# The last 64 rows of d in two weight gradients: half-array pairs in w2's gradient, and the same form at the beginning of w1's

## The chip, the cores and the metric

The kernel runs on one core of a Trainium2 chip. The metric is the device time of one execution in microseconds (us). Three runs of the kernel before took 354.17, 354.51 and 356.31 us; the median is 354.51. The engines are named as in the profile: PE (TensorE, matmuls), PEld (its weight loads), DVE (VectorE), ACT (ScalarE), POOL (GpSimd) and SP (SyncE, which issues most loads).

## The reference

One layer with two branches, forward and backward. The first branch is a layer norm, a real two-dimensional FFT over 2048 x 448, a product with complex weights and the inverse FFT; the second is a layer norm and an MLP over the 2048 tokens.

```python
def _B_ref(x, w1, b1, w2, b2):                      # x: 1 x 2048 x 448
    h = _layernorm(x, axis=-1)
    u = jnp.einsum("bsd,sf->bdf", h, w1) + b1       # f: 1792
    u = _gelu(u)
    y = jnp.einsum("bdf,fs->bds", u, w2) + b2
    return y.transpose(0, 2, 1)

h = x + irfft2(rfft2(_layernorm(x)) * (w_r + 1j * w_i))
h2 = h + _B_ref(_layernorm(h), w1, b1, w2, b2)
_out, _vjp = jax.vjp(f, A_x, A_w_r, A_w_i, B_w1, B_b1, B_w2, B_b2)
```

The kernel returns `h2` and the seven gradients for a given `grad_out`. Two of them matter here, both sums over the 448 values of d: w2's gradient (out_6, 1792 x 2048), the product of gelu(u) and `grad_out`, and w1's gradient (out_4, 2048 x 1792), the product of the normed h and the gradient of u.

## The kernel before

The program is not written in the order in which it runs. Each step is recorded as an operation with the buffers that it reads and writes, the engines that can take it and planned durations; `Plan.order` (from line 266) then lays all operations out by priority, and what each engine gets is a fixed list. Buffers come from rings. The ring "ps" stands for the eight PSUM banks, and `caps` (line 448) limits how many banks each kind of user holds: "mm" 4, "sp" (all transforms) 5, "mw" 8. `_room` (line 211) answers when a further bank of a kind is free. PE's lists keep operations of one "mode" together, since the plan counts 0.095 us for a change between the whole array and halves of it.

The order of the work, roughly: from 0 to 75 us of the span the forward FFT, with products for the gradient of gelu as filler (kind "mg"); to 175 us the two MLP products (kind "mp"); to 219 us the product of w1 with the gradient of u (kind "mm", 16 row tiles), each row followed by the layer norm's backward step `norm_back` on DVE and ACT (lines 1181 to 1207); from 219 to 306 us the backward FFT (`fft_rows`, `fft_cols`, `ifft_cols`, `ifft_rows`, kind "sp"), with w2's gradient as filler; and from 298 us w1's gradient.

Both gradients sum over d = 448, that is three full tiles of 128 rows and 64 rows over. The operands are turned by DMA so that d lies on the partitions: `g_t` and `goT` for w2's gradient, `hlnT` and `du_t` for w1's. Each has four planes of 128 rows; the fourth is loaded from columns 320 to 447, so that its upper half (partitions 64 to 127) holds the last 64 rows of d.

- w2's gradient (lines 1276 to 1285): 14 row tiles of 128, each of four banks of 512 columns. A bank takes four matmuls on the whole array. So that the fourth counts 64 rows alone, POOL zeroes the lower half of `g_t`'s fourth plane (line 1249). ACT moves the banks out.
- w1's gradient (lines 1308 to 1336): 16 row tiles of 128, each of four banks of 448 columns, kind "mw". A bank takes three matmuls on the whole array (`whole`); the last 64 rows run on half of the array (`tails`): a DMA copies the upper half of the fourth plane to the lower half (lines 1250 to 1251), and of two banks one takes its 64 rows from the lower, one from the upper half of the partitions, so that two matmuls run side by side. Even row tiles go whole, whole, tails, odd ones tails, whole, whole, so that the tails of two neighbours meet.

`norm_back` keeps its three small columns (the accumulated sum and two factors) in one tile, "nm". `Norm.moments` (line 705) works in the tile "mv_h", into which the operation before it accumulates.

Of the kernel before, what the change touches and what calls it, by code (L numbers as in the profile page):

```python
# [18 lines left out]
P = 128  # L19
# [118 lines left out]
class Plan:  # L138
# [71 lines left out]
    def _room(self, b, nth):  # L210

        spec = self.rings[b.ring]
        if spec.get("fifo") and spec["next"] + nth != b.seq:
            return None
        ends = sorted(s for s in spec["slots"] if s is not None)
        if len(ends) <= nth:
            return None
        best = ends[nth]
        cap = spec.get("caps", {}).get(b.kind)
        if cap is not None:  # L220
            live = sorted(float("inf") if x.left else x.end for x in spec["live"].get(b.kind, []))
            if len(live) >= cap:
                t = live[len(live) - cap]
                if t == float("inf"):
                    return None
                best = max(best, t)
        return best
# [170 lines left out]
def evict(n):  # L398
    return on_act(n) + on_dve(n)
# [8 lines left out]
def kernel(  # L408
# [39 lines left out]
    ring("ps", 8, ps, fifo=False, caps={"mm": 4, "mg": 2, "sp": 5, "mw": 8, "mp": 6})  # L448
# [24 lines left out]
    ncol = [0]  # L473

# [104 lines left out]
    def turn(j, w2n):  # L579
        for a in range(0, NT, 8):  # L580
            pt = bank("sp", [P, 8, P], BF16)

            def go(e, on, a=a, pt=pt):
                for t in range(8):
                    e.transpose(pt[:, t], w2n[:, (a + t) * P:(a + t + 1) * P], ident[:])

            pl.op(mm(*[128] * 8), go, r=[w2n, ident], w=[pt])
            copy(on_act(1024) + [("DVE", 1.13, 1.21)], lambda a=a: w2T[j][:, a:a + 8, :], lambda pt=pt: pt[:], [pt], [(w2T[j], a)])
# [76 lines left out]
    class Norm:  # L665
# [9 lines left out]
        def stats(self, h):  # L675
            bs = col(6, f"bs_{self.nm}")
            if h % self.by == 0:
                self.mv = col(3 * self.by, f"mv_{self.nm}")
            mv, i, n = self.mv, h % self.by, self.by
            pl.op(on_dve(448, 1.0e-3, 0.07), lambda e, on: e.bn_stats(out=bs[:], in_=self.src[:, h, :]),  # L680
                  r=[(self.src, h)], w=[bs])
            pl.op(small(), lambda e, on: e.bn_aggr(out=mv[:, 2 * i:2 * i + 2], in_=bs[:]), r=[bs], w=[(mv, i)])
            if i == n - 1:
                self.close(h, mv, self.scale)
# [20 lines left out]
        def moments(self, h):  # L705

            mv, i = self.mv, h % self.by
            pl.op(small(), lambda e, on: e.tensor_scalar(
                out=mv[:, 2 * i:2 * i + 1], in0=mv[:, 2 * i:2 * i + 1], scalar1=1.0 / D, scalar2=None, op0=ALU.mult),
                r=[(mv, (i, 0))], w=[(mv, (i, 0))])  # L710
            sq = k1([P, D], "sq")
            pl.op([("ACT", 0.66, 0.8)], lambda e, on: e.activation(
                out=sq[:], in_=self.src[:, h, :], func=ACT.Square, scale=-1.0, bias=mv[:, 2 * i:2 * i + 1],
                accum_out=mv[:, 2 * i + 1:2 * i + 2]), r=[(self.src, h), (mv, (i, 0))], w=[sq, (mv, (i, 1))])
            if i == self.by - 1:
                self.close(h, mv, self.scale / D)
# [37 lines left out]
    def fft_rows(src, zt, g, on_pe):  # L754
# [25 lines left out]
        for i, h in enumerate(hs):  # L780
            pz = bank("sp", [P, 4, 32, 4])
            if on_pe:
                calls = [(512, lambda pz=pz, n=n: pz[0:n], lambda h=h, k=k: src[:, h, parts[k]], signs[k], k == 0, k == 3)
                         for k, n in enumerate((113, 112, 112, 113))]
                matmuls(pz, calls, [(src, h), (src, (h, 1)), kf])
            else:
                matmuls(pz, [(128, lambda c=c, pz=pz: pz[0:DC, c], lambda c=c, i=i: w[:, i, c, :], lambda: kf[:, 0, :],
                              True, True) for c in range(4)], [w, (kf, 0)])
            copy(evict(512), lambda h=h: zt[:, :, :, 4 * h:4 * h + 4], lambda pz=pz: pz[0:DC], [pz], [(zt, h)])
# [3 lines left out]
    def fft_cols(zt, dtab, dst):  # L793
# [4 lines left out]
        def step1(j):  # L798
            pr = bank("sp", [P, 4, DC])
# [20 lines left out]
        def step2(j):  # L820
            px = bank("sp", [P, 2, DF])
# [60 lines left out]
    def ifft_cols(ys, ab):  # L882

        for a in (7, 6, 5, 4, 3, 2, 1, 8):
            two = (a, 16 - a) if a < 8 else (8, 0)
            pa, pb = (bank("sp", [P, 2, 2, 2, 64]) for _ in range(2))
# [42 lines left out]
    def ifft_rows(ab, itab, h):  # L929
        pq = bank("sp", [P, 2, 2, DC])  # L930
# [14 lines left out]
        py = bank("sp", [P, D])  # L945
# [58 lines left out]
    for h in range(NT):  # L1004
        with grouped():
            py = ifft_rows(ab, di0, h)
            if h % nh.by == 0:
                nh.mv = col(3 * nh.by, "mv_h")
            mv, i = nh.mv, h % nh.by
            pl.op([("DVE", 0.54, 0.68)], lambda e, on, py=py, h=h, mv=mv, i=i: e.tensor_tensor_reduce(  # L1010
                out=hn[:, h, :], in0=py[:], in1=hn[:, h, :], scale=1.0, scalar=0.0, op0=ALU.add, op1=ALU.add,
                accum_out=mv[:, 2 * i:2 * i + 1]), r=[py, (hn, h)], w=[(hn, h), (mv, (i, 0))])
            nh.moments(h)
# [167 lines left out]
    def norm_back(pb, xhat, xkey, h, nm, base, out, okey):  # L1181


        nms = col(3, "nm")
# [3 lines left out]
            op1=ALU.add, accum_out=nms[:, 0:1]), r=[pb, xkey, nm.rneg], w=[junk, (nms, 0)])  # L1188
        v = pl.buf("f2", [P, D], "v", F32)
        if nm.raw:  # L1190
            by = 1
            pl.op([("DVE", 0.075, 0.17)], lambda e, on: e.tensor_scalar(  # L1192
                out=nms[:, 1:3], in0=nm.rn[:, h, :], scalar1=nms[:, 0:1], scalar2=None, op0=ALU.mult),
                r=[(nms, 0), (nm.rn, (h, 0)), (nm.rn, (h, 1))], w=[(nms, 1), (nms, 2)])
        else:
            by = 0
            pl.op([("DVE", 0.131, 0.213)], lambda e, on: e.tensor_scalar(
                out=nms[:, 2:3], in0=pb[:, D:D + 1], scalar1=nm.rn[:, h, 0:1], scalar2=-1.0 / D, op0=ALU.mult,
                op1=ALU.mult), r=[pb, (nm.rn, (h, 0))], w=[(nms, 2)])
        pl.op([("ACT", 0.53, 0.64)], lambda e, on: e.activation(  # L1200
            out=v[:], in_=pb[:, 0:D], func=ACT.Identity, scale=nm.rn[:, h, 0:1], bias=nms[:, 2:3]),
            r=[pb, (nms, 2), (nm.rn, (h, 0))], w=[v])
        pl.op([("DVE", 0.595, 0.68)], lambda e, on: e.scalar_tensor_tensor(  # L1203
            out=junk[:], in0=xhat(), scalar=nms[:, by:by + 1], in1=v[:], op0=ALU.mult, op1=ALU.add),
            r=[xkey, (nms, by), v, junk], w=[junk])
# [6 lines left out]
    def ld_t4(t, src, r):  # L1212
        n = t.shape[2]
        ld_parts(t, [0], lambda b: b[:, 0:3, :], lambda: src()[:, 0:384], P * 3 * n * 2, True, r)
        ld_parts(t, [1], lambda b: b[:, 3, :], lambda: src()[:, 320:448], P * n * 2, True, r)

# [4 lines left out]
    ld_t4(goT, lambda: grad_out[0], [])  # L1221
# [27 lines left out]
    pl.op([("POOL", 0.6, 0.7)], lambda e, on: e.memset(g_t[0:64, 3, :], 0.0), w=[(g_t, 1)])  # L1249
    for t in (hlnT, du_t):  # L1250
        st(lambda t=t: t[0:64, 3, :], lambda t=t: t[64:128, 3, :], 64 * t.shape[2] * 4, [(t, 1)], [(t, 2), (t, 1)])

# [22 lines left out]

    for j in range(NFB):
        s6 = pl.buf("w4", [P, S], "s6")
        with grouped():
            for n in range(4):
                pw = product("mm", 512, [(lambda c=c, j=j: g_t[:, c, j * P:(j + 1) * P],  # L1280
                                          lambda c=c, n=n: goT[:, c, 512 * n:512 * n + 512],
                                          [(g_t, c // 3), (goT, c // 3)]) for c in range(4)], [P, 512], hold=s6)
                copy(on_act(512), lambda s6=s6, n=n: s6[:, 512 * n:512 * n + 512], lambda pw=pw: pw[:], [pw], [(s6, n)])
                pl.ops[-1].level = 300.0
# [23 lines left out]
    last = None  # L1308
    for h in range(NT):
        s4 = pl.buf("w4", [P, F], "s4")  # L1310
        bs = [bank("mw", [P, 448]) for _ in range(4)]

        def call(n, rows_, c, start, stop, h=h, bs=bs):
            return (448, lambda: bs[n][:], lambda: hlnT[rows_, c, h * P:(h + 1) * P],
                    lambda: du_t[rows_, c, 448 * n:448 * n + 448], start, stop)

        def whole(h=h, bs=bs, s4=s4):
            return [matmuls(bs[n:n + 2], [call(m, slice(0, P), c, c == 0 and h % 2 == 0,
                                               c == 2 and h % 2 == 1) for m in (n, n + 1) for c in range(3)],
                            [(hlnT, 0), (du_t, 0), (s4, ("held", 0))]) for n in (0, 2)]  # L1320

        def tails(h=h, bs=bs, s4=s4):
            return [matmuls(bs, [call(n + i, (LO, UP)[i], 3, h % 2 == 1, h % 2 == 0) for n in (0, 2) for i in range(2)],
                            [(t, k) for t in (hlnT, du_t) for k in (1, 2)] + [(s4, ("held", 0))], mm(448, 448), "rows")]

        with grouped():
            for o in tails() + whole() if h % 2 else whole() + tails():
                if last is not None:
                    o.soft.add(last.idx)
                last = o  # L1330
            for n in range(4):
                copy(evict(448), lambda s4=s4, n=n: s4[:, 448 * n:448 * n + 448], lambda bs=bs, n=n: bs[n][:], [bs[n]],
                     [(s4, n)])
                pl.ops[-1].level = 300.0
# [52 lines left out]
```

## Time and profile before

| | |
|---|---|
| runs | 354.17, 354.51, 356.31 us, median 354.51 |
| the profiled execution | 354.65 us, span 352.9 us |
| mean granted clock of PE | 0.99 |
| PE waits, by releaser | DMA of w2n 8.7 us (once, at the start), ACT v 4.0 (twice), DVE rneg_x 1.1, and seven under 0.8 |
| evictions of w2's gradient | 56 on ACT, 588 ns each |
| evictions of w1's gradient | 38 on ACT, 538 ns; 26 on DVE, 624 ns |
| `norm_back`'s v on ACT | 725 ns, 16 in the MLP's part |
| zeroing of g_t's half plane on POOL | 1585 ns, once |
| copies of a half plane on POOL's queue | hlnT issued at 252.8 us, landed after 3.7; du_t at 273.0, after 3.5 |

How to read it: the profile is of one execution, made by the hardware profiler, and times are counted from the span's start. A group's line gives what it writes and reads, its shape and count, then its busy time, the mean length of one and the idle time of the engine before it with what ended that. Matmuls overlap in the array: one that lasts 353 ns from start to end can start 190 ns after the one before, so PE's work is read from starts and not from lengths. The chain of waits that ended last is short here: PE with w1's gradient from 306.75 us for 37.83 us, then the last evictions and stores.

### The profile page before, as it was taken

To read this page: it belongs to the slowest core of one execution; us is meant where nothing else is said; L and a number is where in the kernel's file an instruction comes from. 1 tells how busy PE (TensorE), PEld (TensorE's weight loads), DVE (VectorE), ACT (ScalarE), POOL (GpSimd) and SP (SyncE) were. 2 spreads that over 40 slices of the span, in tenths; PEclk is the share of its full clock that TensorE was granted. 3 is DMA by queue.
4 is the path that set the end of the run, shared out by engine and by line. 5 is a ranking of instruction groups with operands and counts; after the bars stand their busy time and mean duration, and the time that the engine had idled before them with its cause. 6 is when DMAs were issued, how large, how long until landed. Compare 5 with 4: busy or idle time off the path is not lost. (4 is left out here: it accounts for less than half of the span.)

```text
span 352.9 us, 6853 instructions
## 1 busy us (share of the span) xinstructions
PE 331.7 (94%) x2507; PEld 180.6 (51%) x2507; DVE 270.4 (77%) x755; ACT 196.8 (56%) x419; POOL 71.7 (20%) x124
## 2 busy tenths in 40 slices
PE   0979999999999999999999999599999999999994
PEld 0546555666655555555555555255555655444441
DVE  5798999886579994422277776859998999997652
ACT  2797833575588776306012222588777887655332
POOL 0000000074701101123220100001111233276522
PEclk9999999999999999999999999699999999999999
DMA  7999799999999999999999999299521555377654
GB/s 239 386 236 210 161 185 298 221 204 294 312 310 316 302 233 306 196 337 261 170 253 241 203 255 248 61 267 236 168 104 81 197 204 201 145 248 246 238 196 156
DMA packets 134685, 80.49 MB, mean 228 GB/s; under 512 B 94268, under 2 KB 127164, under 8 KB 134524
## 3 DMA queue, kind: packets, MB, share of 16 engines
q1 hardware_dynamic: 127148, 52.71, 66.8%
q0 software_dynamic: 7504, 27.35, 22.1%
q8 instruction: 19, 0.31, 0.4%
q14 instruction: 14, 0.11, 0.1%
HBM read 30.98 MB, written 27.08 MB: 165 GB/s over the span
## 5 line engine op out<-in xcount | busy, mean ns | idle before, releaser
L518 PE MATMUL ps_mm<-goT,g_t 128*128 128x512 bf16 x224 | 56.8, 391 | 4.0 <-ACT v L1200 4.0
L518 PE MATMUL ps_mg<-go_n,w2T 128*128 128x448 bf16 x224 | 49.4, 355 | 1.6 <-DMA go_n<-in_grad_out_dram 0.7
L518 PE MATMUL ps_mw<-du_t,hlnT 128*128 128x448 bf16 (+1 forms) x256 | 45.3, 353 | 0.6 <-ACT v L1200 0.5
L518 PE MATMUL ps_mm<-du,w1T 128*128 128x449 bf16 x224 | 43.3, 353 | 0.0
L518 PE MATMUL ps_mp<-hln,w1c 128*128 128x448 bf16 x224 | 42.9, 352 | 0.0
L518 PE MATMUL ps_mp<-gT,w2c 128*128 128x448 bf16 x224 | 42.7, 352 | 0.0
L1200 ACT ACTIVATE v<-ps_mm,nm,rn_h 128x448 f32<-128x448 f32 x16 | 11.6, 725 | 48.7 <-DVE nm L1186 46.7
L508 ACT CAST s<-ps_mm 128x512 bf16<-128x512 f32 x56 | 32.7, 588 | 10.5 <-PE ps_mm L518 10.3
L500 POOL DMA_DIRECT2D out_dram<-s x31 | 16.9, 546 | 91.3 <-ACT s L508 69.1
L518 PEld LDWEIGHTS <-g_t 128*128 128x128 bf16 x224 | 20.3, 100 | 25.3 <-issue 7.4
L518 PEld LDWEIGHTS <-hlnT 128*128 128x128 bf16 (+1 forms) x256 | 20.6, 97 | 24.1 <-issue 6.9
L518 PEld LDWEIGHTS <-w1T 128*128 128x128 bf16 x224 | 21.8, 97 | 21.1
L518 PEld LDWEIGHTS <-w2c 128*128 128x128 bf16 x224 | 21.9, 98 | 20.5
L518 PEld LDWEIGHTS <-w1c 128*128 128x128 bf16 x224 | 21.9, 98 | 20.3
L508 ACT CAST s<-ps_mw 128x448 bf16<-128x448 f32 x38 | 18.6, 538 | 22.9 <-PE ps_mw L518 19.3
L518 PEld LDWEIGHTS <-w2T 128*128 128x128 bf16 x224 | 19.5, 97 | 17.5 <-issue 1.6
L510 DVE CAST s<-ps_mw 128x448 bf16<-128x448 f32 x26 | 15.9, 624 | 10.2 <-PE ps_mw L518 8.3
L1168 DVE SCALAR_TENSOR_TENSOR h<-ps_mp,b2c,hr 128x448 bf16<-128x448 f32 x16 | 9.8, 677 | 16.8 <-PE ps_mp L518 16.8
L816 DVE TENSOR_TENSOR gg<-ps_sp,gb 128x226 bf16<-128x226 f32 x60 | 19.9, 411 | 2.5 <-ACT gb L508 2.5
L1203 DVE SCALAR_TENSOR_TENSOR junk<-hln,nm,v 128x448 bf16<-128x448 bf16 x16 | 10.9, 684 | 11.8 <-ACT v L1200 11.8
L1081 DVE SCALAR_TENSOR_TENSOR ge<-ge 128x448 bf16<-128x448 bf16 x14 | 8.7, 620 | 13.4 <-ACT ge L1079 13.4
L500 POOL DMA_DIRECT2D hn_d<-x x4 | 2.5, 614 | 75.5 <-DVE rn_h L695 71.3
(129 smaller groups left out, 584.1 us busy)
## 6 DMA issues: line engine op xcount, KB each, us to landing
w2c<-in_B_w_dram SPq DMA_DIRECT2D x8, 896.0 KB, 10.6
out_dram<-s POOLq DMA_DIRECT2D x14, 512.0 KB, 3.2
out_dram<-s POOLq DMA_DIRECT2D x15, 448.0 KB, 2.8
w1c<-in_B_w_dram SPq DMA_DIRECT2D x6, 1024.0 KB, 9.3
x<-in_A_x_dram SPq DMA_DIRECT2D x4, 448.0 KB, 7.0
go_n<-in_grad_out_dram SPq DMA_DIRECT2D x2, 896.0 KB, 10.8
hn_d<-x POOLq DMA_DIRECT2D x4, 448.0 KB, 5.8
hln_d<-hln POOLq DMA_DIRECT2D x4, 448.0 KB, 7.4
```

The costliest lines, as they stand in the source:

```text
L500: e.dma_start(out=out() if callable(out) else out, in_=in_())
L508: e.copy(out=out(), in_=in_())
L510: e.tensor_copy(out=out(), in_=in_())
L518: e.matmul(out(), lhsT=lhsT(), rhs=rhs(), start=start, stop=stop)
L816: pl.op(on_dve(226), lambda e, on, s_=s_, op=op: e.tensor_tensor(out=g_[:, s_, :].rearrange("p (k t) -> p t k", t=2), in0=pr[:, 0:2, :], i ...
L1081: gop(stt, [q_, uf], [zz], lambda e, g: e.scalar_tensor_tensor(out=g(zz), in0=g(q_), scalar=6.0 * GELU_C, in1=g(uf), op0=ALU.add, op1=ALU. ...
L1168: pl.op([("DVE", 0.595, 0.68)], lambda e, on, t=t, p2=p2, h2=h2: e.scalar_tensor_tensor(out=h2[:], in0=p2[:, 0:D], scalar=b2c[:, t:t + 1], ...
L1200: pl.op([("ACT", 0.53, 0.64)], lambda e, on: e.activation(out=v[:], in_=pb[:, 0:D], func=ACT.Identity, scale=nm.rn[:, h, 0:1], bias=nms[:, ...
L1203: pl.op([("DVE", 0.595, 0.68)], lambda e, on: e.scalar_tensor_tensor(out=junk[:], in0=xhat(), scalar=nms[:, by:by + 1], in1=v[:], op0=ALU. ...
```

## The change

The core of the diff; the same kind of edit repeated is left out:

```diff
-            if len(live) >= cap:
-                t = live[len(live) - cap]
+            if len(live) + nth >= cap:
+                t = live[len(live) + nth - cap]
...
-    ring("ps", 8, ps, fifo=False, caps={"mm": 4, "mg": 2, "sp": 5, "mw": 8, "mp": 6})
+    ring("ps", 8, ps, fifo=False, caps={"mm": 4, "mg": 2, "sp": 5, "sb": 4, "mw": 8, "mp": 6})
...
-        def moments(self, h):
+        def moments(self, h, sm):
+            if h % self.by == 0:
+                self.mv = col(3 * self.by, f"mv_{self.nm}", bufs=2)
...
-        nms = col(3, "nm")
+        nm2 = col(1, "nm2", bufs=3)
+        ab = col(2, "nm1", bufs=3)
...
-    def ld_t4(t, src, r):
+    def ld_t4(t, src, r, cuts=1):
         n = t.shape[2]
-        ld_parts(t, [0], lambda b: b[:, 0:3, :], lambda: src()[:, 0:384], P * 3 * n * 2, True, r)
         ld_parts(t, [1], lambda b: b[:, 3, :], lambda: src()[:, 320:448], P * n * 2, True, r)
+        for k in range(cuts):
+            at = slice(k * n // cuts, (k + 1) * n // cuts)
+            ld_parts(t, [(0, i) for i in range(4 * k // cuts, 4 * (k + 1) // cuts)], lambda b, at=at: b[:, 0:3, at],
+                     lambda at=at: src()[at, 0:384], P * 3 * n * 2 // cuts, True, r)
+        st(lambda: t[0:64, 3, :], lambda: t[64:128, 3, :], 64 * n * 4, [(t, 1)], [(t, 2), (t, 1)])
...
-    ld_t4(goT, lambda: grad_out[0], [])
+    ld_t4(goT, lambda: grad_out[0], [], 2)
...
-    pl.op([("POOL", 0.6, 0.7)], lambda e, on: e.memset(g_t[0:64, 3, :], 0.0), w=[(g_t, 1)])
-    for t in (hlnT, du_t):
-        st(lambda t=t: t[0:64, 3, :], lambda t=t: t[64:128, 3, :], 64 * t.shape[2] * 4, [(t, 1)], [(t, 2), (t, 1)])
+    sp[0] = "sb"
...
+    behind, EARLY = [], 6
+    def outer(kind, a_t, b_t, j, width, dst, turn, evict_):
+        bs = [bank(kind, [P, width]) for _ in range(4)]
+        held = [(dst, ("held", 0))]
+        begins = (lambda n: n < 2) if turn is None else (lambda n: turn == 0)
+        def call(n, rows_, c, start, stop):
+            return (width, lambda: bs[n][:], lambda: a_t[rows_, c, j * P:(j + 1) * P],
+                    lambda: b_t[rows_, c, width * n:width * n + width], start, stop)
...
+        def tails():
+            return matmuls(bs, [call(n + i, (LO, UP)[i], 3, not begins(n), begins(n)) for n in (0, 2) for i in range(2)],
+                           [(t, k) for t in (a_t, b_t) for k in (1, 2)] + held, mm(width, width), "rows")
+        with grouped():
+            if turn is None:
+                os = [whole(0), whole(1), tails(), whole(2), whole(3)]
+            elif turn == 0:
+                os = [whole(0, 1), whole(2, 3), tails()]
+            else:
+                os = [tails(), whole(0, 1), whole(2, 3)]
+            for o in os:
+                if behind:
+                    o.soft.add(behind[-1].idx)
+                behind.append(o)
...
-            for n in range(4):
-                pw = product("mm", 512, [(lambda c=c, j=j: g_t[:, c, j * P:(j + 1) * P],
-                                          lambda c=c, n=n: goT[:, c, 512 * n:512 * n + 512],
-                                          [(g_t, c // 3), (goT, c // 3)]) for c in range(4)], [P, 512], hold=s6)
+        outer("mm", g_t, goT, j, 512, s6, None, on_act(512))
...
+        outer(*(("mm",) if h < EARLY else ("mw",)), hlnT, du_t, h, 448, s4, None if h < EARLY else h % 2, evict(448))
```

What it does, part by part:

- Both gradients are made by one function, `outer`. In w2's gradient the last 64 rows of d now run as two half-array pairs per row tile: bank 0 whole, bank 1 whole, the tails of all four banks, bank 2 whole, bank 3 whole. `g_t` and `goT` get the copy of the half plane that `hlnT` and `du_t` had; the zeroing of `g_t` goes.
- The first six row tiles of w1's gradient take the same form and the bank kind "mm"; the other ten keep "mw" and the alternation. All row tiles of both gradients stand in one sequence (`behind`).
- The backward transforms have a bank kind of their own, "sb", with four banks instead of five. `_room` counts the banks that the same operation has already asked for.
- `ld_t4` loads the fourth plane first, and `goT`'s first three planes in two pieces.
- The columns of `norm_back` lie in two tiles, those of `moments` apart from the tile that DVE accumulates into, with two to four buffers each.

## The prediction

> **What bounds the kernel now.** I read the page first: busy times, then the slices.
>
> ```profile
> PE 331.7 (94%) x2507; PEld 180.6 (51%) x2507; DVE 270.4 (77%) x755; ACT 196.8 (56%) x419; POOL 71.7 (20%) x124
> ...
> PE   0979999999999999999999999599999999999994
> ...
> PEclk9999999999999999999999999699999999999999
> ```
>
> TensorE (PE) is busy in every slice of 8.8 us but the first, the last and the 26th, where its granted clock also falls. So the end is set by PE's work plus its lost time, and a change is worth what it takes from these two. DVE is busy 53.65 of the 55 us from 245 to 300 (windows), so there the inverse transform is paced by DVE, and PE stays busy only because products fill the gaps. Next, the lines of the groups of instructions for the two gradients that change:
>
> ```profile
> L518 PE MATMUL ps_mm<-goT,g_t 128*128 128x512 bf16 x224 | 56.8, 391 | 4.0 <-ACT v L1200 4.0
> L518 PE MATMUL ps_mw<-du_t,hlnT 128*128 128x448 bf16 (+1 forms) x256 | 45.3, 353 | 0.6 <-ACT v L1200 0.5
> ```
>
> w2's gradient holds PE for 56.8 us; 391 ns is one matmul's length from issue to drained, not its share of the stream. The share comes from the timeline of PE:
>
> ```profile
> 267.85 3.63 PE L518 MATMUL ps_mm<-goT,g_t 128*128 128x512 bf16 x16
> ```
>
> Sixteen starts: (3.63 - 0.39) / 15 = 0.216 us each. w1's gradient already runs its last 64 rows of d in half-array pairs, so its price is in the windows, cut where the form changes:
>
> ```profile
> core 0: us, PE busy (x) PEld busy (x) POOL busy (x), PEclk, DMA share, GB/s
> 312.17:312.83 0.66, 0.66 (x8) 0.20 (x4) 0.00 (x0) 1.00 1.00 402
> 312.83:317.20 4.37, 4.37 (x26) 2.27 (x24) 0.00 (x0) 1.00 0.69 211
> 317.20:317.48 0.28, 0.28 (x2) 0.00 (x1) 0.00 (x0) 1.00 1.02 410
> ```
>
> From 312.83 to 317.20 lie 23 steps of whole-array matmuls, 0.190 us each. From the last of them to the first half-array pair (317.48) it takes 0.28, so going over costs 0.28 - 0.19 = 0.09 us. The first window holds three pairs and the way back: 0.66 = 3 x 0.187 + 0.10. So a pair costs one whole matmul, and each change of form about 0.095 us.
>
> The 26th slice, by windows (columns: window, its length, busy time and count of PE, PEld, DVE, ACT, POOL, clock, DMA):
>
> ```profile
> 220.10:223.50 3.40, 0.99 (x9) 0.62 (x9) 2.43 (x6) 1.23 (x3) 0.00 (x0) 0.99 0.26 90
> 223.50:226.90 3.40, 1.71 (x11) 1.07 (x10) 3.37 (x11) 2.09 (x5) 0.00 (x0) 0.50 0.00 0
> 226.90:230.30 3.40, 3.40 (x11) 1.20 (x9) 3.40 (x10) 2.23 (x5) 0.00 (x0) 0.50 0.92 197
> ```
>
> PE stands still for 4.3 us in two pieces while the last layer-norm backward rows give their banks back, and from 223.5 to 230.3 it runs at half clock. By starts in the trace against the spacings above, 7.1 us are lost from 218 to 235: 4.8 standing, 2.3 to the clock (mostly eight steps of 0.43 instead of 0.216). The last loss is the hand-over to w1's gradient:
>
> ```profile
> 305.70:306.33 0.63, 0.12 (x1) 0.00 (x0) 0.63 (x1) 0.63 (x2) 0.35 (x1) 1.00 0.00 0
> ```
>
> There the steps into 306.33, 306.75 and 307.05 are 0.86, 0.23 and 0.29 us too long: 1.38.
>
> **The change, part by part.** The sum is made against the profiled execution, 354.65 us (span 352.9 and 1.75 around it), 0.14 above the median of the runs, 354.51.
>
> *Pairs in w2's gradient.* In each of 14 row tiles, four whole matmuls on the last rows of d (4 x 0.216) become two pairs (2 x 0.216, at the price that pairs have above) with two changes of form (0.19): 0.242 less each, 3.39 in all. In w1's gradient the first six row tiles no longer alternate and change form twice instead of once: 6 x 0.095 = 0.57 back. In the built order three of these meetings are directly with the transforms' own half-array matmuls, so there are 122 - 91 = 31 changes more, not 34: 28 x 0.216 - 31 x 0.095 = 3.1. PE is the bound on both sides of these tiles, so all of it counts. **-3.1** (bounds -3.4 and 0: no mode costs, or no overlap of pairs with 512 columns, which the trace has only with 448; 448 is the near row).
>
> *A rule that speaks against it.* The spacing above says a change of form costs 0.095 us. The Trainium skill, "TensorEngine Tiling (Array Packing)", section Tiling Modes, says that changing the tiling mode drains TensorE. The trace does not agree with a full drain, which would be 0.353 - 0.19 = 0.163 us here; what that would make of the time stands under the rivals.
>
> *Start of w2's gradient (218 to 235).* DVE takes 2.72 us per layer-norm row there (its accumulation starts at 218.60, 221.32, 224.03), 0.88 of it waiting for ACT's v, and v waits for that accumulation's read-out. Splitting the column tile could have undone this, but in the built order v still waits for the DVE count that the read-out raises. So the 2.72 and PE's two stops stay. What differs is the filling. Before, PE has 12 matmuls of w2's gradient to run from 226.8 while DVE folds the third group; after, six stand before those folds, because a row tile now goes bank, bank, tails, bank, bank and waits behind the next folds. These six run out at 225.6 (full clock) to 226.9 (half), and the third group's folds end at 228.46 in the trace: 0.3 to 2.9 us of standing, middle 1.6. Against it, less work falls under the half clock: 1.4 or less is lost instead of 2.3. **+0.5** (bounds -2.3, no half clock; +2.2, one more stretch of 3.4 us at half clock, which costs 1.7).
>
> *Hand-over to w1's gradient.* Before, a row tile asks for four banks at once, and from 298 on nearly all wait until the transform is through. After, six row tiles are of the kind that w2's gradient has and in the built order 96 of their matmuls stand among the last seven rows of the transform and behind it; the rest follow with no stop in which four banks must come free. **-1.3** of the 1.38 (bounds -1.4 and 0).
>
> *The order of the forward transform (43 to 74)* changes too: the bank count now counts both banks that one operation asks for, and the norm's columns have buffers of their own. Six short waits lose 1.5 us there, the largest 0.40 at 64.6 for DVE's merge, where two products' filler now stands. **-0.7** (bounds -1.5 and +0.6).
>
> *Four banks instead of five for the backward transform*, against other waits of 0.6 us in 235 to 300: **-0.2** (bounds -0.6 and +1.5).
>
> *At nothing.* The zeroing of g_t's lower half goes (POOL, 1.58 us; POOL stands 13.8 before and 37 after it). Instead POOL issues copies of 0.54 us for g_t and goT in that same gap of 37. goT's load in two pieces adds one issue of some 0.6 us on SP; it lands near 211 and is needed at 222.9; df, w_b, di and xr behind it were issued by 213.8 and are needed from 235. Without those covers each costs its own 0.5 to 0.6. POOL's copies for hlnT and du_t wait for transposes that before had long landed (hlnT's by 238.5 against a copy at 252.8), so stores queued behind them wait for nothing. The column tiles add no instruction.
>
> Sum: -3.1 + 0.5 - 1.3 - 0.7 - 0.2 = -4.8, so 349.85 by the profiled execution, **349.7 us** by the median.
>
> **The rivals.**
>
> *The half clock lasts one stretch more or less.* Before, it held for two stretches of 3.4 us. After, PE is nearly idle from 219 to 227, longer than before, so a third is possible: +1.7, 351.4. Or one falls wholly into standing time and costs nothing: -1.4, 348.3. The Trainium skill, "TensorE: Matmul & The Clock Gate", Part 1, says that the window of about 3.4 us runs freely, so that where it lies differs between executions; no run here shows that yet.
>
> *Every change of form costs a full drain*, 0.163 us: 31 x 0.163 = 5.1, so the pairs bring 6.05 - 5.1 = 1.0 instead of 3.1: 351.8. The steps of 0.28 speak against it.
>
> *Only PE's work shrinks*, and the waits move instead of going: -3.1 + 0.5 and the rest nothing: 351.9. For it: DVE is full from 245 to 300 in both kernels.
>
> *Slower: four banks starve the backward transform.* Each of its steps needs one bank to write and others being read by ACT (0.353) and DVE (0.39); w2's tiles hold all four of theirs from the tails to four evictions on ACT (0.588 each). If PE then waits one eviction, 0.59, at each of 16 rows and 8 column groups, it loses 14 us: 359. It decides from 4.8 / 24 = 0.2 us a step; over 1% slower from 0.35. Against it: before, two w2 tiles of banks were in use beside the transform and such waits came to 0.6 us in all.
>
> *The pairs do not overlap* with 512 columns: 28 x 0.216 comes back: 355.8. Against it: the first window above.
>
> **How the numbers follow.** Forecast 0.56; longer half clock 0.15, shorter 0.13; drain 0.03; only the work 0.07; starved 0.04; no overlap 0.02. The range takes in the forecast and both clocks with the bound of the banks, 347.9 to 352.0. A measurement of this kernel can tell about 1%, 3.5 us, so faster means below 351.0. Of the forecast 0.93 lies there (it would need 1.3 us more), of the shorter clock all, of the longer clock a fifth: 0.52 + 0.13 + 0.03 = 0.68. Slower: the starved case, 0.04. Same: 0.28.
>
> **What would show it.** Right: w2's matmuls as 168 whole and 56 half ones, a pair every 0.216, steps of about 0.31 into and out of it; PE's busy time down by some 3; no stop of PE at the beginning of w1's gradient; a stop before the third group's folds near 226. Wrong: PE waiting among the transform's rows from 235 to 300 for more than 1.5 us in all, a half clock beyond 234, or changes of form above 0.12 us.

## The result, and the profile after

The changed kernel took 351.47 us (median of six runs, 350.74 to 356.95), timed beside the kernel before (356.12, 354.17 to 356.31): a ratio of 0.990, 95% interval 0.9868 to 0.9932, so 3.5 us of 354.5; the medians lie 4.65 us apart. The ratio leaves out slow runs, those more than 1.5% above a kernel's fastest (here the one of 356.95). Timed again the ratio came to 0.9949 (0.9912 to 0.9986; run *again* below). The kernel is faster, by 0.5 to 1%, and by the ratio that is less than the 4.8 us that were forecast. The kernel before scatters too: beside the experiments most of its runs lie between 353.1 and 357.9 us, and no trace shows what its longer ones wait for. One thing is odd: the profiled execution took 354.71 us (span 352.9), as long as the profiled one of before, while four of the other runs took 350.74 to 351.54. The profile says why. The page first, busy times and the slices of 8.8 us:

```profile
PE 327.8 (93%) x2507; PEld 175.8 (50%) x2507; DVE 271.4 (77%) x758; ACT 194.5 (55%) x416; POOL 70.9 (20%) x125
...
PE   0979999997899999999999999499999999999994
...
PEclk9999999999999999999999999879999999999999
```

PE works 3.9 us less than before (331.7), yet the span is the same: there are new holes in the 10th and 11th slices, about 86 us. The groups of the two gradients (the words after the bar: busy time, mean ns):

```profile
L519 PE MATMUL ps_mm<-goT,g_t 128*128 128x512 bf16 (+1 forms) x224 | 51.5, 387 | 0.0
...
L519 PE MATMUL ps_mw<-du_t,hlnT 128*128 128x448 bf16 (+1 forms) x160 | 27.7, 353 | 0.0
...
L519 PE MATMUL ps_mm<-du_t,hlnT 128*128 128x448 bf16 (+1 forms) x96 | 18.0, 354 | 0.0
```

w2's gradient went from 56.8 to 51.5 us, w1's from 45.3 to 27.7 + 18.0 = 45.7. What PE waited for, two of the lines (us in total, times, longest):

```profile
PE ps_sb L519 <- ACT v L1202: 5.0, 3, 2.3
PE ps_mg L519 <- DMA w2T<-in_B_w_dram: 3.7, 2, 2.9
```

The second line holds the hole (2.9; the other 0.8 lies at 48 us, for an earlier one of these loads). The timeline of PE around it (start, length, operation, count, and the idle time ahead with what ended it):

```profile
85.87 0.54 PE L519 MATMUL ps_mg<-go_n,w2T 128*128 128x448 bf16 x2
89.26 2.44 PE L519 MATMUL ps_mg<-go_n,w2T 128*128 128x448 bf16 x12 [2.85 <-DMA w2T<-in_B_w_dram]
```

In the forward part PE's filler, the products for the gradient of gelu, ran out of operands: the last of the transposed loads of w2 landed at 89.2. The start of w2's gradient and the hand-over to w1's, by windows (columns as in the prediction):

```profile
218.00:235.00 17.00, 11.94 (x82) 7.15 (x81) 13.88 (x39) 7.84 (x15) 0.52 (x1) 0.80 0.79 189
305.70:306.33 0.63, 0.63 (x11) 0.57 (x10) 0.63 (x2) 0.00 (x0) 0.33 (x1) 1.00 0.70 278
```

The second window, in which PE ran 0.12 of 0.63 us before, is now full. The first is no better than before (12.82 us busy there, the same clock of 0.80). And two pairs among the transform's matmuls:

```profile
234.40 0.61 PE L519 MATMUL ps_mm<-goT,g_t 64*128 64x512 bf16 x4
234.94 0.77 PE L519 MATMUL ps_sb<-kf,w 128*113 128x128 bf16 x10
```

Four half-array matmuls take 0.61, of which 0.38 is the length of the last: the second pair starts 0.23 after the first, and the transform 0.31 after that.

The table has PE's lost time by stretch in us, worked out for each trace as the prediction did: the steps between starts less the spacings of 0.216 (512 columns), 0.189 (448) and 0.095 for a change of form. *Work* is the sum of these spacings. The kernels of the lower rows are described under the experiments.

| trace | work | 43–74 | 74–96 | 96–175 | 218–235 | 235–300 | 300–310 |
|---|---|---|---|---|---|---|---|
| before | 320.1 | 2.0 | 0.2 | 0.0 | 7.1 | 1.5 | 1.5 |
| changed | 317.1 | 1.7 | 3.3 | 0.0 | 8.2 | 1.7 | 0.4 |
| again | 317.1 | 1.3 | 0.3 | 4.3 | 7.9 | 1.9 | 0.4 |
| w2t_first | 317.1 | 1.3 | 0.2 | 0.1 | 8.2 | 1.4 | 0.4 |
| before_count | 320.6 | 1.4 | 0.2 | 0.0 | 8.4 | 1.8 | 1.0 |
| early_0 | 316.7 | 1.3 | 0.2 | 0.0 | 8.6 | 1.2 | 2.4 |
| v_first | 317.3 | 1.3 | 6.4 | 0.0 | 3.2 | 1.4 | 0.4 |

### The profile page after: what moved, and what is told of

It reads as the page before. It is cut to its first block, busy times and chain, and to the rows that moved or that the text cites. A ratio compares the mean times of both kernels' runs of the same rounds, so it can differ in the third digit from the quotient of the medians.

```text
span 352.9 us, 6854 instructions
## 1 busy us (share of the span) xinstructions
PE 327.8 (93%) x2507; PEld 175.8 (50%) x2507; DVE 271.4 (77%) x758; ACT 194.5 (55%) x416; POOL 70.9 (20%) x125
## 5 line engine op out<-in xcount | busy, mean ns | idle before, releaser
L519 PE MATMUL ps_mg<-go_n,w2T 128*128 128x448 bf16 x224 | 50.3, 355 | 5.3 <-DMA w2T<-in_B_w_dram 3.7
L519 PE MATMUL ps_mm<-goT,g_t 128*128 128x512 bf16 (+1 forms) x224 | 51.5, 387 | 0.0
L509 ACT CAST s<-ps_mm 128x512 bf16<-128x512 f32 (+1 forms) x72 | 38.8, 587 | 7.8 <-PE ps_mm L519 7.2
L519 PE MATMUL ps_mw<-du_t,hlnT 128*128 128x448 bf16 (+1 forms) x160 | 27.7, 353 | 0.0
L519 PEld LDWEIGHTS <-g_t 128*128 128x128 bf16 (+1 forms) x224 | 15.8, 98 | 20.1 <-issue 8.7
L1205 DVE SCALAR_TENSOR_TENSOR junk<-hln,nm,v 128x448 bf16<-128x448 bf16 x16 | 11.0, 685 | 11.5 <-ACT v L1202 11.5
L509 ACT CAST s<-ps_mw 128x448 bf16<-128x448 f32 x21 | 10.7, 533 | 16.3 <-PE ps_mw L519 12.2
L519 PE MATMUL ps_mm<-du_t,hlnT 128*128 128x448 bf16 (+1 forms) x96 | 18.0, 354 | 0.0
L519 PEld LDWEIGHTS <-kinv 128*128 128x128 bf16 x192 | 14.6, 97 | 6.4 <-DVE eo L945 2.4
```

The source lines that it names most:

```text
L509: e.copy(out=out(), in_=in_())
L519: e.matmul(out(), lhsT=lhsT(), rhs=rhs(), start=start, stop=stop)
```

## The experiments

Every kernel was timed beside the kernel before on the same chip (355.1 to 355.7 us by median); ratios are to that. Where nothing else is said the edit is made to the changed kernel.

### The pairs of w2's gradient: tails_whole and tails_whole_w2t_first

```diff
+            if width == 512:
+                return matmuls(bs, [call(n, slice(0, P), 3, not begins(n), begins(n)) for n in range(4)], ...)
             return matmuls(bs, [call(n + i, (LO, UP)[i], 3, not begins(n), begins(n)) ...
```

with the zeroing of `g_t`'s lower half put back in place of the two copies.

> Undoes the half-array pairs of w2's gradient alone: the four tails of a row tile are four matmuls on the whole array (with the zeroed lower half of g_t's fourth plane), at the same place in the row tile, the four banks and everything else as in the changed kernel. Theory A (PE's work bounds, and the price of the prediction holds): 28 x 0.216 comes back and 28 changes of form at 0.095 go, +3.4 us: about 354.8 against 351.4. Theory B (PE's work is not the bound there; the waits take it up): within 0.8 of 351.4. It also shows the forward part a second time, since the order before the layer norm's backward rows is the changed kernel's: if the stop of about 3 us for w2T at 86 us belongs to the order, it is there again; if it belongs to one execution, it is not.

Measured: 359.65 us, 356.44 to 361.73, ratio 1.0119 (1.0066 to 1.0171). The direction is theory A's, the size can't be read: this trace has the hole at 86 us too (2.5 us for w2T), with the clock at half behind it. So it was repeated once the hole was gone (the load moved as in *w2t_first*, below):

> The half-array pairs of w2's gradient undone once more, now without the disturbance at 86 us. Theory A (PE's work counts in full: 321.06 - 317.07 by the spacings, 21 changes of form less and 28 matmuls of 0.216 more): +4.0, 355.5 against 351.46. Theory B (the pairs' gain is partly taken up by waits): 352.5 to 354.

Measured: 355.41 us, ratio 1.0013 (0.999 to 1.0035), against 351.46 and 0.9881 with the pairs: 3.95 us by the medians, 4.7 by the ratios. So theory A: PE's work counts in full. That the medians meet the forecast so closely is in part luck, since in this trace the half clock between 218 and 235 us also lasted longer (0.70 of full speed, 0.80 in *w2t_first*). The ratio of 1.0013 also says that without the pairs the change is worth nothing: what its other parts win and lose adds up to zero.

### The beginning of w1's gradient: early_0

```diff
-    behind, EARLY = [], 6
+    behind, EARLY = [], 0
```

> Undoes the first six row tiles of w1's gradient alone: all sixteen are of kind mw and alternate, as in the kernel before. Theory A (the beginning in w2's form removes the stop at the hand-over): the loss of 1.1 to 1.4 us between 305 and 308 us comes back and four to six changes of form (0.095 each) go: +0.6 to +1.0, about 352.2 against 351.4. Theory B (the stop went for another reason, say the order of the transform's last rows): no stop there and the changes of form saved, about 351.0. Forward part as in the changed kernel: the same question on w2T's stop.

Measured: 353.43 us, ratio 0.9975 (0.994 to 1.001); seven of twelve runs at 352.5 to 353.6, where the changed kernel's four shorter runs have 350.7 to 351.5. Against its second timing (*again* below, 353.19 us, eight runs at 351.5 to 354.0) the times alone would not decide; the trace does, for theory A, and the loss is larger than expected. What PE waited for, three of the lines:

```profile
PE ps_sb L519 <- DVE eo L945: 0.8, 1, 0.8
...
PE ps_mw L519 <- DVE s L511: 0.3, 1, 0.3
PE ps_mw L519 <- ACT s L509: 0.2, 1, 0.2
```

From 300 to 310 us PE loses 2.4 instead of 0.4. So the stop does not go with the old order of the transform's last rows: it comes back with the kind "mw". That these row tiles may ask for all eight banks while the transform still needs its own is the likely reason; it was not tried by itself.

### Four banks or five: sb_5

```diff
-    ring("ps", 8, ..., caps={"mm": 4, "mg": 2, "sp": 5, "sb": 4, "mw": 8, "mp": 6})
+    ring("ps", 8, ..., caps={"mm": 4, "mg": 2, "sp": 5, "sb": 5, "mw": 8, "mp": 6})
```

> One number: the backward transforms may hold five banks instead of four. Theory A (the cap hardly matters, as the prediction's small term has it): 350 to 352. Theory B (the tails hold four banks of a row tile at once, and five for the transform make nine of eight): PE stops among the transform's rows from 235 to 300 us, an eviction or two (0.588 each) at each of 14 row tiles, 8 to 16 us: 359 to 368.

Measured: 384.85 us, ratio 1.0809 (1.0744 to 1.0875): beyond theory B. The trace, windows and waits:

```profile
235.00:300.00 65.00, 46.17 (x544) 29.59 (x546) 61.25 (x167) 36.49 (x82) 8.26 (x16) 0.82 0.51 125
```

```profile
PE ps_sb L519 <- DVE eo L945: 9.7, 10, 1.6
...
PE ps_sb L519 <- DVE gg L819: 4.3, 3, 2.4
```

PE is busy 46 of 65 us there (64.8 in the changed kernel), at a granted clock of 0.82, and what it waits for most are DVE's operations on the transform's banks (eo, gg). That fits five and four banks asked of eight; the edit shows that the fifth bank costs this, not by which wait it begins. The prediction had a rival in which four banks starve the transform; it is five that do.

### The start of w2's gradient: v_first and whole_first_w2t_first

```diff
-            out=junk[:], in0=pb[:, 0:D], in1=xhat(), scale=nm.rneg[:, h:h + 1], ..., accum_out=nm2[:])
...
             out=v[:], in_=pb[:, 0:D], func=ACT.Identity, scale=nm.rn[:, h, 0:1], bias=ab[:, 1:2])
+            out=junk[:], in0=v[:], in1=xhat(), scale=nm.back, ..., accum_out=nm2[:])
```

> The accumulated sum of the layer norm's backward row is taken over v (which ACT writes to SBUF) instead of over PE's bank; the sum is the same up to rounding, since the normed row adds up to zero. So v no longer stands behind DVE's pass over the bank, and the bank is free after v alone. Theory A (PE's two stops and the half clock between 218 and 235 us come from DVE's 2.72 us per row, 0.88 of it waiting for v, and from v's waiting for the accumulation): the last three rows each end 0.9 earlier, the stops shrink by 2.7 to 4 us: 347.4 to 348.7 against 351.4. Theory B (what PE waits for there is DVE's folding work or the filler, whatever the rows do): within 1 us of 351.4.

Measured: 351.84 us, 349.69 to 358.14, ratio 0.9883 (0.9843 to 0.9923). The time alone would speak for theory B. The trace doesn't; the window from 218 to 235, to be held against the changed kernel's above:

```profile
218.00:235.00 17.00, 14.48 (x143) 8.85 (x143) 12.83 (x36) 10.87 (x20) 0.53 (x1) 1.00 1.03 215
```

PE works 14.48 us instead of 11.94, at the full clock instead of 0.80; the loss there is 3.2 instead of 8.2. It comes otherwise than theory A had it: the last rows are no shorter (v starts every 2.87 us, and still waits for DVE's short step on the bank's last column). But from the first v to the last of the 16 it takes 41.3 instead of 45.9 us, so that the last v ends 2.4 us behind PE's last product of w1 with the gradient of u instead of 7.6. This execution also loses 6.4 from 74 to 96 us: 4.3 waiting for w2T and the rest to half clock behind it. The gain was real and the hole hid it, as the last kernels show.

The other edit, made to *w2t_first*, asks whether PE stood there for lack of matmuls that may go. Which matmul begins a bank's sum is changed to match:

```diff
-                os = [whole(0), whole(1), tails(), whole(2), whole(3)]
+                os = [whole(0, 1), whole(2, 3), tails()]
```

> In w2's gradient and the first six rows of w1's, all four banks go whole first and the tails of all four come last; so twelve matmuls instead of six stand ahead of the third group's folds near 226 us. Theory A (the prediction's step: PE stands there for lack of matmuls that may go): six more of 0.216, the stop shorter by up to 1.3: 350.2 against 351.46. Theory B (PE's stop is set by when the layer norm's rows give banks and operands, whatever fills it; and with the tails last all four banks of a row tile end together, so that four evictions of 0.588 stand between one row tile and the next): no gain there, and from 235 to 300 up to 14 x 0.59 = 8 more: 355 to 360.

Measured: 359.31 us, ratio 1.0106 (1.0074 to 1.0138). The first half of the question stays open: in the built order six matmuls stand ahead of the third group's folds again (224.57 to 227.08 in the trace), not twelve, and from 218 to 235 PE loses 8.2 us as in *w2t_first*. The second half is theory B's. The windows behind:

```profile
235.00:300.00 65.00, 60.70 (x597) 31.82 (x596) 60.07 (x155) 45.30 (x99) 12.41 (x23) 1.00 0.70 174
300.00:310.00 10.00, 7.57 (x61) 4.11 (x60) 10.00 (x32) 7.13 (x15) 5.30 (x10) 1.00 0.66 225
```

In *w2t_first* PE is busy 63.92 and 9.88 us in these two. So the order bank, bank, tails, bank, bank earns its place; that it does so by spreading the four evictions is the likely reason, not shown by itself.

### The hole at 86 us: again, room_old, w2t_first, before_w2t_first, before_count

> The changed kernel once more, unaltered, for a second trace and more times. Its first trace stops 2.9 us at 86 us of the span for the last transposed load of w2T; four kernels with the same forward order showed it in three of four traces, and times in two groups some 3.5 to 5.5 us apart. Theory A (the stop is part of this order and comes and goes with the landing of that load, 11 us after its issue or 7.5): two groups again, about 351 without it and 354.5 to 357 with it. Theory B (the first trace was an exception): one group, 350.7 to 351.6.

Measured: 353.19 us, ratio 0.9949 (0.9912 to 0.9986); twelve runs, eight at 351.5 to 354.0 and four at 355.7 to 356.6: two groups, as theory A had it, although less sharp. But theory A's cause is not borne out: the trace, of a run of 355.96 and so of the longer group, has no hole at 86. It has one at 150 us, again behind a late load; the waits of PE, and of ACT in the 30 us from 120:

```profile
PE ps_mp L519 <- DVE gT L1086: 2.4, 1, 2.4
```

```profile
ACT gb2j L1176 <- DMA go_r<-in_grad_out_dram: 10.2, 1, 10.2
```

ACT's list holds the sums over `go_r` (line 1176) in a fixed place; their load is late, all of ACT stands behind it, then DVE's gT, then PE for 2.4 us and some 1.9 at half clock. ACT has one wait of 9 to 11.5 us for that load in every trace. In all it waits 18.7 us for it here, 12.7 to 16.8 in the others, and here alone it reached PE. So of the six longer runs of the changed kernel (two of six, then four of twelve) two were traced, each with another load late; what the other four waited for isn't shown.

The one line that gave the forward part its new order, undone:

```diff
-            if len(live) + nth >= cap:
-                t = live[len(live) + nth - cap]
+            if len(live) >= cap:
+                t = live[len(live) - cap]
```

> Undoes one line of the change, the count of banks that an operation has already asked for. With it the whole forward part, up to the layer norm's backward rows, is laid out instruction by instruction as in the kernel before; pairs, four banks, hand-over and column tiles stay. Theory A (the stop for w2T comes from the new forward order): no stop at 86 us in the trace, losses of PE from 43 to 74 of 2.0 as before (0.7 more than the other four traces of the new order), times in one group, 350.7 + 0.7 = about 351.5. Theory B (the stop comes and goes with the DMA whatever the order): it is seen in this trace or in a third of the times, 3 to 6 us above the rest.

Measured: 358.61 us, ratio 1.0075 (1.0036 to 1.0113). Both theories fail on the time, and A on the trace too. The hole at 86 is there, with the old order (PE waits 3.4 for w2T). And PE's last matmul starts at 347.9, as in the changed kernel, but the span is 358.1: the last products of the spectral weights' gradient come after everything else. Timeline of DVE at the end:

```profile
348.32 0.62 DVE L511 CAST s<-ps_mw 128x448 bf16<-128x448 f32 x1 [0.46 <-PE ps_mw L519]
351.95 0.52 DVE L869 TENSOR_TENSOR gw<-t_r,t_i 128x675 bf16<-128x675 bf16 x1 [3.00 <-DMA out_dram<-gw]
```

So undoing this line alone can't be read from the time: it also moves work that no part of the prediction had followed. What can be moved alone is a load:

```diff
     ld_w1(2, 0, 4)
     for j in range(10, 12):
         ld_w2T(j)
-    ld_w1(4, 4, 7)
     for j in range(12, 14):
         ld_w2T(j)
+    ld_w1(4, 4, 7)
```

> The new forward order with one load moved: w1's columns for the second block (two issues, 1.5 MB) are issued behind the last two transposed loads of w2T instead of ahead of them. Theory A (the last transposed load lands late because it is issued late, 76 to 78 us, behind the issue and the traffic of these 1.5 MB): it is issued some 2 us or more earlier, lands before 84, no stop at 86, one group of times at about 351. Theory B (that load is slow for another reason, or the stop has another cause): it lands 10 us or more behind its issue again, and the two groups stay. What can go wrong on its side: w1's columns land later and PE waits for them at 95 to 105 us, which the trace would show.

Measured: 351.46 us, all six runs between 350.38 and 352.62, ratio 0.9881 (0.9839 to 0.9923). Theory A. The last two transposed loads, by the DMA view of a stretch about their issue (count, median us from issue to landing), in the changed kernel and in this one:

```profile
w2T<-in_B_w_dram SPq DMA_TRANSPOSE x2, 10.5
```

```profile
w2T<-in_B_w_dram SPq DMA_TRANSPOSE x2, 6.7
```

They are issued at 65.8 and 71.4 instead of 70.2 and 78.0, the last lands at 78 instead of 89, and PE waits for none of them; w1's block is not missed. None of the four later traces with this load moved and the new order shows the hole either. What sets it off is the landing of the last transposed load, by its own issue and landing in each trace. Where it wasn't moved it took 10.4 to 12.5 us in the five traces with the hole and 5.6 to 8.5 in the five without, the kernel before among them (7.3).

The kernel before with the same edit, and with the count of banks alone:

> The kernel before with the same single load moved as in w2t_first (w1's second block behind w2T's last two transposed loads); PE, DVE, ACT and POOL keep their order, four issues on SP change places. Theory A (a late w2T costs the kernel before too, less often): one group of times at its undisturbed level, 353.2 to 354.7; against w2t_first's 351.5 the change is then worth 2 to 3.3 us. Theory B (the late load is a matter of the changed kernel alone): 355.1 to 356.1, as the kernel before has been timed, and w2t_first is 4 us better.

Measured: 355.5 us, ratio 0.9997 (0.9977 to 1.0017): theory B. The kernel before had no such cost to speak of. In its first trace, with the load unmoved, that load landed at 83.3 and was first used at 85.3: 2 us to spare.

```diff
-            if len(live) >= cap:
-                t = live[len(live) - cap]
+            if len(live) + nth >= cap:
+                t = live[len(live) + nth - cap]
```

> The kernel before with one line of the change alone: the count of banks that an operation has already asked for. It gives the kernel before the changed kernel's forward order, instruction by instruction on every engine, up to the layer norm's backward rows; pairs, four banks and hand-over are not in it. Theory A (this order brings w2T's last load to the edge): the 43 to 74 us stretch loses 0.7 less, but executions some 3 to 6 us longer come in a third of the cases, and the median is not better than the kernel before's (ratio 1.000 to 1.012, wider spread). Theory B (the late load has nothing to do with the order; room_old had it too): one group, 0.7 faster, ratio 0.998. In both: PE's loss from 218 to 235 tells whether the 1.0 us more that the changed kernel loses there comes from this line (8.2 instead of 7.1) or from the pairs' filling (7.1).

Measured: 355.92 us, ratio 1.0016 (0.9983 to 1.005); eight of twelve runs at 354.5 to 356.2, four at 357.5 to 358.4. This one line, then: 0.6 us less lost from 43 to 74, nothing gained in time. That the order brings the hole about is not shown. The trace is of one of the four longer runs (357.73) and has no hole at 86, and the kernel before beside it ranges from 353.1 to 361.2 itself. Of the traces whose load wasn't moved, four of seven of the new order have the hole and one of three of the old (*room_old*); the load was issued at 76.2 to 78.3 us in the seven and at 74.0 to 77.9 in the three, so no later start sets them apart. The trace does show the other half. The window from 218 to 235:

```profile
218.00:235.00 17.00, 11.77 (x90) 7.60 (x89) 13.05 (x36) 9.57 (x17) 0.54 (x1) 0.80 0.77 180
```

PE is busy 11.77 us, less than in the changed kernel, and loses 8.4, without any pair in it. The stops of PE, by its timeline (the idle time ahead and what ended it stand in the brackets), in the kernel before and in this one:

```profile
222.89 0.59 PE L518 MATMUL ps_mm<-goT,g_t 128*128 128x512 bf16 x2 [2.33 <-ACT v L1200]
225.59 1.01 PE L518 MATMUL ps_mm<-goT,g_t 128*128 128x512 bf16 x2 [1.69 <-ACT v L1200]
```

```profile
222.16 0.38 PE L518 MATMUL ps_sp<-kf,w 128*113 128x128 bf16 x4 [0.81 <-ACT v L1200]
224.88 0.22 PE L1347 MATMUL ps_mm<-ident,gb1b 128*14 128x128 bf16 x1 [2.33 <-ACT v L1200]
227.57 0.58 PE L518 MATMUL ps_sp<-kf,w 128*113 128x128 bf16 x4 [1.83 <-ACT v L1200]
```

Two things make the standing longer. The layer norm's rows trail more: the last v ends 7.6 us behind PE's last product of w1 with the gradient of u, 7.0 in the kernel before, and the first stop grows by about as much (0.81; 0.16 before, not shown). And between the two long stops the kernel before runs two matmuls of w2's gradient (2 x 0.216 us); here none run, and a further stop of 0.26 stands there. In sum these waits are 4.2 us before and 5.2 here, with the old form of w2's gradient. The changed kernel has 5.0 and v 7.6 behind; *room_old*, with the new form and the old order, has 4.0 and 7.0. So the longer standing goes with the bank count's new order and not with the pairs.

### Both edits: v_first_room_old, v_w2t_first and v_w2t_first_2

> Both edits together: the sum of the layer norm's backward row taken over v, and the old count of banks (the old forward order). v_first lost 3.2 us from 218 to 235 where the changed kernel lost 8.2, and 6.2 at 86. Theory A (the two are independent, and the stop at 86 belongs to the new order): 351.4 - 5.0 + 0.7 = about 347, in one group, faster than the kernel before by 2%. Theory B (the stop stays, or the gain at 218 is given back in the transforms): 349 or more.

Measured: 351.4 us, 349.5 to 362.91, ratio 0.9857 (0.9801 to 0.9912). Its trace has no hole, loses 1.2 us from 218 to 235, and PE starts its last matmul at 337.7, ten before that of the changed kernel; but the span ends at 347.7, with the same late products as *room_old*. Theory A's 347 isn't reached: four runs lie at 349.5 to 352.6 and two at 361.0 and 362.9. Then the two edits that don't touch the bank count, *v_first* and *w2t_first*:

> The changed kernel with two edits: the sum of the layer norm's backward row over v, and w1's second block behind w2T's last loads. Theory A (the stops at 218 to 235 and at 86 are independent): 351.46 less the 5.0 us by which v_first lost less from 218 to 235: 346.5, at most 348 if the half clock comes in some executions; under 0.98 of the kernel before. Theory B (given back in the transforms behind, where DVE is full): 350 or more.

Measured: 347.06 us, ratio 0.9748 (0.9717 to 0.978). Theory A. Once more, for the trace and more times:

> The best kernel so far once more, for a trace of an undisturbed execution and more times: 345.7 to 347.5, ratio 0.972 to 0.978; the trace should lose 3 to 3.5 us from 218 to 235 without half clock, nothing at 86, and end PE at about 340.

Measured: 346.99 us, ratio 0.9754 (0.9709 to 0.9799): the best kernel of the study, 2.5% under the kernel before. Nine of the twelve runs took 345.7 to 348.1 us and three 351.3 to 355.4. Both traces are of longer ones (355.39 and 352.5), so the undisturbed trace that was wanted is missing, and two of the readings expected of it did not come: the clock from 218 to 235 is 0.90, and PE's last matmul starts at 345.9. Nothing is lost at 86. What disturbed the second is a wait of ACT, and PE behind it for 3.8 us:

```profile
ACT s L509 <- DMA out_dram<-s: 4.7, 1, 4.7
```

a store of w2's gradient that had not landed when its buffer was wanted. In the first ACT waits for such stores too (6.4 us in three waits). That is what is late next.

## Why the prediction was right or wrong

*PE work, -3.1: right.* The work by spacings fell from 320.1 to 317.1, -3.0, and undoing the pairs cost 3.95 us of time where the spacings gave 4.0. The price of a pair was taken over from 448 to 512 columns; a pair takes 0.226 in the trace, 0.01 more than was put down. A change of form held at 0.095. The rivals of the full drain and of pairs that don't overlap are out.

*Hand-over, -1.3: right, and sized well.* The stretch from 300 to 310 us loses 0.4 instead of 1.5, -1.1. Undoing it alone gave back 2.0 there.

*Order of the forward transform, -0.7: the step that failed.* It was priced by the waits of PE among the transform's steps alone. These shrank as forecast (1.3 or 1.4 instead of 2.0 in six traces of the new order; in the changed kernel's first, 0.8 of waiting for w2T lies in the same stretch). It left out, without a reason, what the same order does elsewhere. The order lengthens PE's stops from 218 on, where *before_count* loses 8.4 instead of 7.1 with nothing else changed. And the forward part hangs on a load: the last transposed one of w2T had 2 us to spare before, less than the spread of its landing. In the profiled execution it came late, and PE lost 3.1 us at 86. That the margin was too small is shown, by moving the load; that the new order made it smaller is not. In sum the line with the bank count is worth nothing (1.0016). The prediction did list, for goT, who waits for which load and how long it has landed; for the forward part it followed no load at all.

*Start of w2's gradient, +0.5: the sign right, the mechanism in part, the size 0.6 short (+1.1).* The rows stay at 2.72 us, since v waits behind DVE's accumulation; with the sum taken over v 5 us of the loss went. PE does lack filler, as forecast, and its waits there grew by 0.8 us. But the six matmuls do not run out ahead of the third group's folds: in the changed kernel they start at 229.86, behind the last stop, and the folds follow them without one. And the lack was put down to the new row tile of bank, bank, tails, bank, bank, while *before_count* stands as long with the old row tile.

*Four banks, -0.2: about nothing (+0.2), and the risk was on the other side*, as *sb_5* showed.

So without the late load the trace gives -3.0 - 1.1 - 0.7 + 1.1 + 0.2 = -3.5 (1.1 being 8.2 less 7.1), and 354.65 - 3.5 = 351.1 is where the four undisturbed runs lie. The forecast of 4.8 is 1.3 too much, of which the start is 0.6, the banks 0.4 and the hand-over 0.2. The late loads come on top; a third of the executions are longer, and in the two of them that were traced it was a load. That the median of 351.47 lies as near the forecast as it does owes something to this split: with one longer run more among the six it would be near 353.

*Slips in the working.* The starved rival's 14 us, added to the forecast, give 364 and not 359. The standing at 226, between ends of 225.6 to 226.9 and 228.46, is 1.6 to 2.9 us and not 0.3 to 2.9. The upper end of the range, the longer half clock with the bound of the banks, is 353.1 and not 352.0. And the third slice of PE, at seven tenths, also stands out, besides the three that are named.

*The clock.* The rival of one stretch more or less of half clock happened in neither direction in the profiled execution: 0.80 of the window from 218 to 235 in both, two stretches of 3.4 us.

## What to carry to other kernels

A change of the order of work moves every transfer's due time as well as every engine's: list the loads that the moved stretch consumes, with the time from landing to first use, and treat a margin under the spread of a load's landing (here 5.6 to 12.5 us after issue for one load, with 2 us to spare) as a cost that comes in some executions. When a kernel's times fall into groups and a trace shows a wait that others don't, give that load its slack first and measure afterwards: the same edit (*v_first*) read as nothing by the medians with the late load (351.84 against 351.47), and as 4.4 us without (347.06 against 351.46). And an instruction that only shares a bank with a reduction can wait for it, as v did here; taking the sum from ACT's copy in SBUF ended that wait.

## What the runs showed of the hardware that was not expected

A short stop of PE can cost the clock, and a longer one need not. Behind the hole at 86 us, in the trace of *tails_whole*:

```profile
89.12 3.90 PE L519 MATMUL ps_mg<-go_n,w2T 128*128 128x448 bf16 x12 [2.45 <-DMA w2T<-in_B_w_dram]
```

Twelve matmuls take 3.90 us after a stop of 2.45, while in the changed kernel, shown above, the same twelve take 2.44 after a stop of 2.85. The granted clock from 86 to 96 us was 0.83 in the one and 1.00 in the other, and 1.00 behind a stop of 3.40 in *room_old*. The length of the stop alone does not decide it. The Trainium skill, "TensorE: Matmul & The Clock Gate", Part 1, says that the clock gate watches activity over a window of about 3.4 us that runs freely. It also says there that the half clock comes after at least one idle window of that length; with a stop of 2.45 us in front of the half clock this trace does not agree, and the measurement decides. That it depends on where in such a window the stop lies would fit all three stops, but no run here shows where the windows lay.
